# Cosformer attention and MLP-mixer on one core: loading q of batch 4 ahead of its k and v, and q of batch 5 half a period later

## The chip, the cores and the metric

The kernel runs on one core of a Trainium2 chip. The core has a matrix engine (PE, with a row PEld for its weight loads), a vector engine (DVE), a scalar engine (ACT), a general engine (POOL) and SyncE (SP), which here only issues DMAs. The DMAs that SP issues all go out on one hardware queue (q1 in the profile); the stores that POOL issues go out on another (q0). Time is device time in microseconds (us), the median of several runs of the whole program.

## What is computed

For each of 8 batches there are 8 heads of 576 tokens and 64 dimensions. The attention is linear:

```
phi(x) = [relu(x)*cos(theta_s), relu(x)*sin(theta_s)]        theta_s = pi/2 * s/576
kv  = phi(k)^T v          z = sum_s phi(k)                    per head: 128 x 64, 128
x   = phi(q) kv / (phi(q) z + 1e-6)                           576 x 512 per batch
h   = relu(x^T w_tok1) w_tok2                                 token mixing, 576 -> 256 -> 576
u   = x + h^T
out = u + relu(u w_ch1) w_ch2                                 channel mixing, 512 -> 1536 -> 512
```

## The kernel before

**Tiling.** The 576 tokens of a batch are laid out as five tiles (`j` = 0 to 4, `NJ` = 5): four full tiles of 128 tokens, and a tail of 64 that is paired with the tail of the neighbouring batch. A batch of q, k or v is loaded in float32 by `load` (L132) in two DMAs, one of 512 KB for the even partitions and one of 640 KB for the odd ones. Both go through SP.

**Periods.** After a head that works through the first batches, the kernel is a row of periods `g` = 1 to 8, each a list of steps. Period `g` runs channel mixing of batch `g` on PE (`mlp1` at L312, 12 steps, then the second product: `mlp2` at L330 in period 1, `mlp2_unit` at L374 from period 2, a seven-product Strassen-Winograd form on halves whose operand sums are made on DVE by `s_sums`, L354 to L357). Between these products it weaves in the attention and the token mixing of batch `b` = `g`+1 (`num_step`, `b1_step`, `u_step`, `uturn_step`), and the features and the kv product of batch `f` = `g`+2. Counting the head's period `g` = 0 as the first, `g` = 1 is the second period and `g` = 2 the third. Periods are named by `g` from here on.

**Order.** No scheduler moves anything. `plan_of(g)` puts calls into steps with `put(step, function, ...)`, and the calls of a step are issued after that step's matrix product. An engine runs its instructions in the order in which they were issued, and starts one when the semaphores that it waits for are there. So the step number sets the place in each engine's row, and the row, with the waits, sets the time.

**What the steps around the change do.** For batch `f`:

- `q_load`, `k_load`, `v_load` issue the two DMAs of a tensor on SP.
- `qfeat` makes phi(q): the cosine half on DVE (L140), the sine half on ACT (L138). `qturn_dma` (L162) transposes the result by a DMA that SP issues.
- `f1k` makes one half of phi(k), on DVE or ACT (the same lines).
- `vcast` turns a tile of v into bfloat16 on POOL (L156).
- `kv_step` multiplies them on PE (L183), at steps 20 to 25.

For batch `b`, `u_step` adds the token mixing to x on DVE (L255); `uturn_step` casts u on ACT (L260) and transposes it by a DMA on SP (L265). PE needs that transpose, `uT`, for the first product of the next period. `tail_step` and `tail_turn` (L291, L300) handle the paired tails, where `b` is odd. The evictions of `mlp1` to `h1T` are mostly on ACT (L324), in order with its share of `qfeat` and `f1k`.

**Buffers.** q has two raw buffers (batch parity). From batch 4 on, k and v have one raw buffer each, since the second ones then hold the sums of the second product. So a load of v(5) waits until POOL has cast v(4), and a load of v(6) until it has cast v(5).

Of the kernel before, what the change touches and what calls it, by code (L numbers as in the profile page):

```python
# [18 lines left out]
def kernel(  # L19
# [528 lines left out]
    A, V, G = nc.scalar, nc.vector, nc.gpsimd  # L548
# [370 lines left out]
    def plan_of(g):  # L919
        b, f = g + 1, g + 2  # L920
        NS = 24 if g == 1 else 26
        plan = [[] for _ in range(NS)]

        def put(s, fn, *args):
            plan[s].append(lambda: fn(*args))

        if g == 1:
            put(5, tail_step, 1)
            put(19, tail_turn, 1)
            for j in range(NJ):  # L930
                put(j // 2 + 1, f1k, b, j, 0, V)
                put((j + 1) // 2 + 2, kv_step, b, j)
                put(5 + j, num_step, b, j)
            put(3, u_out, 1, 1)
            for n in range(2):
                put(10 + n, b1_step, b, n)
                put(13 + n, u_step, b, n)
                put(13 + n, uturn_step, b, n)
            for j in range(NJ):
                put(8 + j, f1k, f, j, 1, A)  # L940
                put(10 + j, f1k, f, j, 0, V)
                put(8 + j, vcast, f, j, G)
                put(18 + j, kv_step, f, j)
            for j, at in enumerate((12, 15, 16, 17, 18)):
                put(at, q_step, f, j)
            for i in range(4):
                put(19 + i, t_sum, i)
            put(8, v_load, 4)
            put(20, q_load, 4)
            put(22, k_load, 4)  # L950
            return plan
        if b < B:
            for j in range(NJ):
                put(2 + j, num_step, b, j)
            for n in range(2):
                put(8 + n, b1_step, b, n)
                put(12 + n, u_step, b, n)
                put(15 + n, uturn_step, b, n)
            put(18, tail_step, b)
        for at, cs in ((7, (0, 2)), (9, (2, 4)), (11, (4, 5))):  # L960
            put(at, s_sums, *cs)
        if f < B:
            for j in range(NJ):
                put((7, 8, 10, 12, 13)[j], qfeat, f, j, V, A)
                put((7, 8, 10, 17, 17)[j], qturn_dma, f, j)
                put((12, 13, 14, 15, 17)[j], f1k, f, j, 0, V)
                put(13 + j, f1k, f, j, 1, A)
                put(j, vcast, f, j, G)
                put((20, 21, 22, 24, 25)[j], kv_step, f, j)
        if f + 1 < B:  # L970
            put(0, q_load, f + 1)
            put(6, v_load, f + 1)
            put(18, k_load, f + 1)
        return plan

    for g in range(1, B + 1):
        mps = {}
        plan = plan_of(g)
        order = order_of(g)
        for s in range(len(plan)):  # L980
            if s < NCH:
                ps = mlp1(g, order[s])
            elif g == 1:
                t, part = divmod(s - NCH, 3)
                if part == 0:
                    mps[t] = nextM()
                mlp2(g, t, part, mps[t])
            else:
                mlp2_unit(g, s - NCH)
                mlp2_sums(g, s - NCH)  # L990
            for fn in plan[s]:
                fn()
            flush()
            if s < NCH:
                mlp1_out(order[s], ps, V if s in ((11,) if g == 1 else (10,)) else A)
                if g > 1 and s == NCH - 1:
                    s_sums(NQ - 1, NQ)
            elif g == 1 and part == 2:
                mlp2_out(g, t, mps[t], False)
# [33 lines left out]
```

## Time and profile before

| what | value |
|---|---|
| time, median of 5 runs | 263.04 us (263.0 to 263.6) |
| the profiled execution | 263.6 us, its span 261.8 us |
| PE busy | 251.8 us (96% of the span) |
| DVE, ACT, POOL busy | 187.8, 148.2, 97.9 us |
| granted clock of PE | full in all 40 slices |
| DMA | 57.18 MB, mean 218 GB/s |
| one q, k or v batch by SP | 512 KB and 640 KB, median 7.5 to 10.1 us from issue to landing |

A row of the timeline gives start and duration in us, the engine, the line, the operation, what it writes and reads, and how many were merged; the brackets at its end tell how long the engine stood idle before it, and what ended that. A row "SPq" is the time in which SP issues a DMA, not the transfer. In the chain of waits each line is a start, a duration, and the work or wait that the end hangs on at that time.

The periods begin on PE at 87.01 (`g` = 2), 114.62 (`g` = 3), 141.07 (`g` = 4), 167.57 (`g` = 5) and 193.59 us (`g` = 6).

### The profile page before, as it was taken

The numbers are of one execution on the slowest core, as the hardware profiler recorded it, in microseconds if no ns is written. First come the engines' busy times: TensorE is split into PE (matmuls) and PEld (weight loads), VectorE is DVE, ScalarE is ACT, GpSimd is POOL, SyncE is SP. The second block draws the span as 40 slices with busy tenths as digits, with TensorE's granted clock in tenths as the row PEclk, the third lists the DMA queues.
The fourth block names the chain that finished last, engine by engine and source line by source line (L and its number), as shares of the span: only waits on it lengthen the run. The fifth ranks groups of instructions, "written<-read, shape, count | busy, mean of one in ns | idle before, by whom it ended". The sixth has DMA issues, their size and how long they took to land.

```text
span 261.8 us, 5609 instructions
## 1 busy us (share of the span) xinstructions
PE 251.8 (96%) x2074; PEld 154.3 (59%) x2074; DVE 187.8 (72%) x447; ACT 148.2 (57%) x246; POOL 97.9 (37%) x175
## 2 busy tenths in 40 slices
PE   7799999999999999999999999999999999999994
PEld 2465456555545554875586557755875576486483
DVE  5794767696969688939993999489939773563563
ACT  4564586885576429845792679367935452613610
POOL 5178466161142510392039402830291045045041
PEclk9999999999999999999999999999999999999999
DMA  6999999999987999999999997985381034003004
GB/s 193 367 373 384 388 390 384 322 211 262 374 255 168 247 236 356 270 199 326 353 192 147 330 342 157 203 271 100 65 215 70 3 80 162 18 3 150 13 0 162
DMA packets 79947, 57.18 MB, mean 218 GB/s; under 512 B 48176, under 2 KB 74928, under 8 KB 79920
## 3 DMA queue, kind: packets, MB, share of 16 engines
q1 hardware_dynamic: 76128, 47.26, 67.5%
q0 software_dynamic: 2560, 8.39, 9.1%
q10 hardware_dynamic: 1232, 1.18, 1.4%
q8 instruction: 16, 0.26, 0.4%
q14 instruction: 11, 0.09, 0.1%
HBM read 35.85 MB, written 9.44 MB: 173 GB/s over the span
## 4 chain that ended last, share of the span: by engine, by line
PE 67%; DMA 5%; ACT 2%; issue 1%; SPq 1%; DVE 0%; ACTq 0%
PE psM L312 27%; PE psM L374 21%; PE psA L232 4%; PE psM L330 4%; PE psA L250 4%; DMA q_raw<-in_q_dram 3%; PE psA L183 2%; PE psA L207 2%; DMA uT<-u_bf 2%; PE psA L291 1%; ACT u_bf L260 1%; ACT h1T L324 1%; PE psA L374 1%; ACT kp L138 0%; SPq L132 0%
## 5 line engine op out<-in xcount | busy, mean ns | idle before, releaser
L312 PE MATMUL psM<-uT,w_ch 128*128 128x512 bf16 x368 | 88.0, 379 | 0.4 <-DMA uT<-u_bf 0.4
L324 ACT ACTIVATE h1T<-psM 128x512 bf16<-128x512 f32 x93 | 55.4, 597 | 42.6 <-PE psM L312 40.7
L312 PEld LDWEIGHTS <-w_ch 128*128 128x128 bf16 x416 | 38.1, 97 | 40.7 <-issue 0.7
L392 POOL TENSOR_TENSOR res<-res,u_sb 128x256 f32<-128x256 f32 x36 | 26.7, 768 | 78.1 <-DVE res L397 77.7
L156 POOL CAST vb<-v_raw 128x512 bf16<-128x512 f32 (+1 forms) x43 | 23.9, 598 | 23.2 <-DMA v_raw<-in_v_dram 22.8
L138 ACT ACTIVATE kp<-k_raw,sin_t 128x512 bf16<-128x512 f32 (+1 forms) x45 | 28.1, 667 | 1.1 <-DMA k_raw<-in_k_dram 1.1
L138 ACT ACTIVATE qp<-q_raw,sin_t 128x512 bf16<-128x512 f32 (+1 forms) x40 | 26.3, 682 | 4.3 <-DMA q_raw<-in_q_dram 4.3
L374 PEld LDWEIGHTS <-h1T 128*128 128x128 bf16 x252 | 23.8, 97 | 6.2 <-issue 0.6
L374 PEld LDWEIGHTS <-k_raw 128*128 128x128 bf16 x252 | 24.4, 98 | 5.1 <-issue 1.2
L330 PE MATMUL psM<-w_ch,h1T 128*128 128x512 bf16 x96 | 23.8, 379 | 0.0
L374 PE MATMUL psM<-w_ch,h1T 128*128 128x256 bf16 x168 | 22.3, 273 | 0.6 <-ACT h1T L324 0.6
L140 DVE TENSOR_SCALAR kp<-k_raw,cos_t 128x512 bf16<-128x512 f32 (+1 forms) x45 | 20.5, 483 | 1.7 <-DMA k_raw<-in_k_dram 1.7
L255 DVE TENSOR_TENSOR u_sb<-psA,x_sb 128x1024 f32<-128x1024 f32 x16 | 19.5, 1219 | 1.7 <-PE psA L250 1.5
L207 PEld LDWEIGHTS <-qpT 128*128 128x128 bf16 x320 | 14.9, 98 | 9.7 <-issue 1.6
L374 PE MATMUL psM<-w_ch_t,k_raw 128*128 128x256 bf16 x162 | 20.5, 273 | 0.0
L223 DVE TENSOR_TENSOR x_sb<-psA,rden 128x512 bf16<-128x512 f32 x28 | 19.4, 691 | 1.0
L140 DVE TENSOR_SCALAR qp<-q_raw,cos_t 128x512 bf16<-128x512 f32 (+1 forms) x40 | 16.7, 449 | 3.9 <-DMA q_raw<-in_q_dram 3.9
L354 DVE TENSOR_TENSOR k_raw<-h1T 128x512 bf16<-128x512 bf16 (+1 forms) x28 | 9.9, 354 | 11.8 <-ACT h1T L324 11.1
L250 PE MATMUL psA<-B,w_tok 128*128 128x512 bf16 x64 | 16.4, 379 | 0.0
L440 POOL DMA_DIRECT2D out_dram<-res x16 | 8.9, 558 | 19.4 <-DVE res L335 13.6
L219 DVE TENSOR_SCALAR rden<-psA 128x8 f32<-128x8 f32 x35 | 5.7, 163 | 13.7 <-PE psA L207 13.4
L193 ACT CAST kv_sb<-psA 128x520 bf16<-128x520 f32 x7 | 4.2, 603 | 18.9 <-PE psA L183 18.9
(134 smaller groups left out, 378.5 us busy)
## 6 DMA issues: line engine op xcount, KB each, us to landing
out_dram<-res POOLq DMA_DIRECT2D x32, 256.0 KB, 3.5
k_raw<-in_k_dram SPq DMA_DIRECT2D x7, 640.0 KB, 8.6
v_raw<-in_v_dram SPq DMA_DIRECT2D x7, 640.0 KB, 10.1
q_raw<-in_q_dram SPq DMA_DIRECT2D x7, 640.0 KB, 10.0
k_raw<-in_k_dram SPq DMA_DIRECT2D x7, 512.0 KB, 7.5
v_raw<-in_v_dram SPq DMA_DIRECT2D x7, 512.0 KB, 10.0
q_raw<-in_q_dram SPq DMA_DIRECT2D x7, 512.0 KB, 9.4
u_sb<-in_moe_w_ch_dram SPq DMA_DIRECT2D x2, 1024.0 KB, 10.2
```

Source lines behind the costliest of these rows:

```text
L138: eng.activation(out_ap, in_ap, AF.Relu, bias=0.0, scale=s)
L140: eng.tensor_scalar(out_ap, in_ap, scalar1=s, scalar2=0.0, op0=ALU.mult, op1=ALU.max)
L156: eng.tensor_copy(out_ap, in_ap)
L207: nc.tensor.matmul(dst, w, kv_sb[:, h, 0:E1], start=True, stop=True, skip_group_check=True)
L223: nc.vector.tensor_mul(dst.rearrange("p (g h d) -> p g h d", g=2, h=HH), n[:, :, :, 0:D], rb)
L250: nc.tensor.matmul(ps[:, half, :], w2[:, ki, 2 * c + half, :], B1[b % 2][:, ki, :], start=(ki == 0), stop=(ki == NT - 1))
L255: nc.vector.tensor_add(u_sb[b % 2][:, 2 * c:2 * c + 2, :], ps, x_sb[:, 2 * c:2 * c + 2, :])
L312: nc.tensor.matmul(ps.rearrange("p (t k) -> p t k", k=P), wc1[:, ki, mi * P:(mi + 1) * P], src[:, :, ki, :], start=(ki == 0), stop=(ki == ...
L324: eng.activation(h1T[:, mi, :], ps, AF.Relu)
L330: nc.tensor.matmul(ps, h1T[:, ki, t * P:(t + 1) * P], wc2[:, ki, :], start=(ki == 0), stop=(ki == NCH - 1))
L374: nc.tensor.matmul(m[tt][:, tt, :], a[:, c, tt * P:(tt + 1) * P], w[:, c, :], start=(pr < 4 and c == 0 and (tt == 0 or own)), stop=(c == N ...
L392: G.tensor_add(c[:, t, :], s[:, t, :], u[:, t, :])
```

## The change

In period 1, q of batch 4 is loaded at step 8, where v of batch 4 was; k and v of batch 4 are loaded at step 20. In period 2, q of batch 5 is loaded at step 8 instead of step 0, and v of batch 5 at step 18 (ahead of k of batch 5) instead of step 6; the five casts of v of batch 4 are issued at step 12 instead of steps 0 to 4. Periods 3 to 8 keep their plan. Nothing else changes: the instructions on PE, DVE and ACT and their order are the same, on POOL the five casts come behind the two tail copies (L283), and on SP the loads take other places.

```diff
@@ plan_of, g == 1
                 put(at, q_step, f, j)
             for i in range(4):
                 put(19 + i, t_sum, i)
-            put(8, v_load, 4)
-            put(20, q_load, 4)
-            put(22, k_load, 4)
+            put(8, q_load, 4)
+            put(20, k_load, 4)
+            put(20, v_load, 4)
             return plan
@@ plan_of, g > 1
                 put((12, 13, 14, 15, 17)[j], f1k, f, j, 0, V)
                 put(13 + j, f1k, f, j, 1, A)
-                put(j, vcast, f, j, G)
+                put(j if g > 2 else 12, vcast, f, j, G)
                 put((20, 21, 22, 24, 25)[j], kv_step, f, j)
         if f + 1 < B:
-            put(0, q_load, f + 1)
-            put(6, v_load, f + 1)
+            put(8 if g == 2 else 0, q_load, f + 1)
+            put(18 if g == 2 else 6, v_load, f + 1)
             put(18, k_load, f + 1)
         return plan
```

SP's row before, from the end of period 1: turn of the tails, q(4), k(4), q(5), v(5), turns of q(4) tiles 0, 1, 2, turn of u in two halves, turns of q(4) tiles 3 and 4, turn of the tails, k(5), then in period 3 q(6), v(6), turns of q(5). After: turn of the tails, k(4), v(4), turns of q(4) tiles 0 and 1, q(5), turn of tile 2, turn of u in two halves, turns of tiles 3 and 4, turn of the tails, v(5), k(5), then q(6), v(6), turns of q(5).

## The prediction

> **What bounds the kernel now.** I read the page first. PE is busy for 96% of the span at full clock in every slice, so time can only come out of the few places where PE stands. To find them I cut the span at the starts of the periods and asked for the busy time of each stretch; the columns are length, then PE, PEld, DVE, ACT and POOL busy with counts.
>
> ```profile
> PE 251.8 (96%) x2074; PEld 154.3 (59%) x2074; DVE 187.8 (72%) x447; ACT 148.2 (57%) x246; POOL 97.9 (37%) x175
> ...
> 87.01:114.62 27.61, 27.01 (x236) 17.14 (x234) 22.15 (x53) 16.43 (x27) 9.40 (x15) 1.00 1.11 270
> 114.62:141.07 26.45, 26.02 (x231) 17.19 (x232) 21.03 (x51) 17.09 (x28) 9.94 (x17) 1.00 1.10 253
> 141.07:167.57 26.50, 26.50 (x234) 17.15 (x235) 20.99 (x52) 16.92 (x28) 10.58 (x17) 1.00 1.05 250
> 167.57:193.59 26.02, 26.02 (x237) 17.20 (x234) 20.77 (x51) 16.64 (x27) 9.42 (x16) 1.00 0.67 167
> ```
>
> Periods 2 and 4 hold the same work on PE (both have a tail step), yet 2 takes 27.61 us and 4 takes 26.50: period 2 loses 1.11 us. Periods 3 and 5 are the pair without a tail step: 26.45 against 26.02, so period 3 loses 0.43. The chain of waits says what period 2 lost it to.
>
> ```profile
> 88.99 0.61 ACT h1T L324
> 89.60 0.46 SPq L300
> 90.06 0.05 issue
> 90.11 1.26 SPq L132
> 91.37 0.06 issue
> 91.42 6.85 DMA q_raw<-in_q_dram
> ```
>
> q(4) is issued at 90.11 and 91.42, behind the turn of the tails on SP, and lands at 91.42 + 6.85 = 98.27. The timelines of ACT and PE show who stands meanwhile.
>
> ```profile
> 94.23 0.60 ACT L324 ACTIVATE h1T<-psM 128x512 bf16<-128x512 f32 x1 [0.45 <-PE psM L312]
> 98.38 0.72 ACT L138 ACTIVATE qp<-q_raw,sin_t 128x512 bf16<-128x512 f32 x1 [3.55 <-DMA q_raw<-in_q_dram]
> ...
> 101.22 0.71 PE L374 MATMUL psM<-w_ch,h1T 128*128 128x256 bf16 x5 [0.31 <-ACT h1T L324]
> 102.20 0.28 PE L374 MATMUL psM<-w_ch,h1T 128*128 128x256 bf16 x1 [0.27 <-ACT h1T L324]
> ...
> 141.07 2.75 PE L312 MATMUL psM<-uT,w_ch 128*128 128x512 bf16 x12 [0.43 <-DMA uT<-u_bf]
> ```
>
> The first sine half of q(4) holds ACT for 3.55 us, and the evictions of h1T queue behind it. PE has four banks to run ahead in, so it stands only at the second product. The rest of the loss of period 3 is in the last row: a wait for uT.
>
> **The change, part by part.**
>
> *q(4) at step 8 of period 1.* Removed from the path: the wait for q(4). SP issued v(4) at 66.10 to 69.58 in this place, and its two halves took 9.8 and 10.0 us to land, so q(4), of the same sizes, should be there by 79, and nothing asks for it before 94.8. The raw buffer of q(2) has long been read by then. What period 2 gains is read against period 4, stage by stage on PE's timeline: start of period to first L374, 14.21 against 13.73 (0.48 us); that to the first L250, 1.10 against 0.65 (0.45); from there to the first L183, 7.63 in both; from it to the end, 4.67 against 4.49 (0.18). Sum 1.11 us. The last 0.18 is a wait for the turn of u, which is late because ACT is late: the casts of u end 21.95 us into period 2 and 21.07 into period 4. With ACT on time the turn of u's second half is issued at 87.01 + 21.1 = 108.1. Such a turn landed after 2.7 us in period 4 and after 5.2 in period 3, so it lands at 110.8 to 113.3, before the clean end of the period, 87.01 + 26.50 = 113.51. Gain: **1.11 us**, bounds 0.93 (the 0.18 stays) and 1.11.
>
> *k(4) and v(4) at step 20.* SP reaches them where q(4) and k(4) were, at 90.1 and 92.2, so they land as those did: k(4) by 98.3, and v(4), by k(4)'s rows (92.92 plus 8.6), by 101.5. The first feature of k(4) is wanted at about 103.6 and the first kv product at 108.8. Cover of 5 us for k; v has its five casts in between (2.83 us in a row in the later periods), and they end near 104.5. If the load were 4 us later this cover would be gone and PE would wait at L183. Cost 0.
>
> *q(5) at step 8.* It now stands between the turns of q(4) tiles 1 and 2. Those turns depend on the queue: the turn issued at 100.11 held SP for 4.70 us and took 8.8 to land with q(5) and v(5) ahead of it, and the third was issued only at 107.95. After the change only v(4) is ahead of the first one, which is ready at about 97.4; q(5) goes out near 102 and lands by about 107, and SP is free again well before the turn of u at 106.5 (its two halves each 1.2 to 1.3 us). q(5) is not needed before 122. Cost 0, bounds 0 and 0.5 (tile 2's turn holding up the turn of u as it did at 107.95 to 109.19).
>
> *The casts of v(4) at step 12.* They leave 83.61 to 91.6, where one of them held a DVE sum (1.53 us against 0.95 for its equal at L341), but no PE wait hung on that. They now run at about 101.6 to 104.5, beside DVE's busiest stretch. What a POOL operation costs DVE is seen at 95.97: L355, with both inputs in SBUF, took 0.72 instead of 0.42 beside a copy. A feature (L140) took 0.68 instead of 0.48 beside casts at 73.51; evictions from PSUM kept their 0.69. Some 1.1 us of operand sums and two features fall into these casts, so DVE is late by at most 1.1 + 0.4 = 1.5 us. The sums have 1.15 us in hand (in period 3 S2 is done at 130.24, its product starts at 131.39), the casts of u 1.25 (second L255 ends 133.41, its cast on ACT starts at 134.66). Cost 0, upper end 0.3.
>
> *v(5) at step 18, and v(6) behind it.* SP comes to v(5) at about 113.6 (period 4: the turn of the tails ends 26.5 us into it), 4.6 us before it came to k(5), 118.20. It shares the engines with four stores and the turn of the tails, so it lands at about 121. POOL, free at 115.5, waits for it and casts until about 124: no one needs these casts before the kv product at 134.9. But two things follow. First, the casts meet the operand sums of period 3 (122 to 124): four sums by 0.30 and two features by 0.20 make 1.6 us, against 0.36 us of DVE's own idle time before L326 and the 1.15 in hand. I take **0.1 us**; the ends are 0 and, with DVE shut out for all 2.1 us, 0.6. Second, v(6), at step 6 of period 3, waits for the casts, and behind it on SP stand the turns of q(5) and the turn of u(4) that period 3 already waits for. v(6) was issued at 122.06 to 124.0 and landed at 122.76 + 10.1 = 132.9; now it is issued at 124 to 126. That by itself is hidden: k(5) and q(6) are in the queue ahead of it and land about 3.3 us apart (129.6 and 132.9 before), and all started 4.6 us earlier with one load more (3.3). So v(6) should land at 131 to 132.5. The turns of q(5) wait for room in the queue as before, and the turn of u starts when its cast is done, 19.5 and 21.1 us into the period. The wait for uT stays at about 0.4. Cost **0**, ends -0.43 (the wait goes, since that turn took 5.2 us where others took 2.7 to 2.9) and +2.5 (v(6) casts and turns all late).
>
> *A rule against the change.* The Trainium skill, page SBUF — State Buffer, section "SBUF: two separate sides", says that POOL and DVE share one port pair as an exclusive lock, held for a whole instruction, against DVE operations with two SBUF inputs. Its 1.53 us row agrees: 0.58 more beside one cast of 0.62. By the rule the casts of v(5) would take all of the 2.1 us named above, and the sum would be 0.5 us less gain; the rows at 95.97 and 73.51 show a part only.
>
> The sum: -1.11 + 0.1 = -1.0 us. The profiled execution took 263.6 us, span 261.8 and 1.8 around it; by the sum it becomes 262.6. It lies 0.56 above the median of the runs, 263.04, so the median becomes **262.0 us**.
>
> **The rivals.** A measurement of this kernel can tell about 0.2%, 0.53 us, from no change: faster means under 262.5, slower over 263.6.
>
> *DVE eats the gain.* Both sets of casts shut DVE out (0.3 in period 2, 0.6 in period 3), the 0.18 stays: -1.11 + 0.3 + 0.6 + 0.18 = 0.0 at worst, typically -0.3. For it: DVE is busy for nearly all of 122 to 137. Against: 1.15 to 1.6 us in hand in both places. Time 262.6 to 263.1. To this case belongs that the change moves the wait without removing it, with ACT held by something else in its place; nothing on ACT's row before 94.8 suggests one.
>
> *Slower: SP stands at v(6).* v(5) lands late, its casts end late, and the turn of u(4) is caught behind v(6) and the turns of q(5). Clean, period 3 would start at 113.51 and be through with PE's work at 113.51 + 26.02 = 139.53. To lose the 1.11 and 0.53 more, PE must start period 4 at 141.07 + 0.53 = 141.6, so uT must land at 141.46. From the last load's landing to the issue of the second half of u there are a turn of q(5) and the first half (2.5 us), and its landing takes 2.7 to 5.2: v(6) must land after 133.8 to 136.3, that is v(5) some 2 to 4 us later than I have it. For it: the wait exists already and has no slack, and every further us is paid in full. Against: the 4.6 us of head start. Time 263.6 to 265, say 264.2.
>
> *A larger gain.* The uT wait of period 3 goes too: 262.0 - 0.43 = 261.6. It belongs to the forecast's own range, 261.4 to 262.5.
>
> **How the numbers follow.** The forecast has 0.65, DVE (or another wait) eating the gain 0.17, SP standing at v(6) 0.18. Faster 0.65, the same 0.17, slower 0.18. The range goes from 261.3 (both waits gone) to 263.8, which leaves out about 0.03 below and 0.14 of the slower case above.
>
> **What would show it.** Right: ACT goes from the seventh L324 of period 2 to L138 on q(4) without idle time; no PE row of L374 near 101 waits for h1T; period 2 is 26.4 to 26.7 us long; the casts of v(4) start at 101 to 102; v(6) is issued at 124 to 126 and period 3 is 26.0 to 26.6 long. Wrong: L374's third product pair waits for DVE's S2 in period 2 or 3; PE waits for uT at the start of period 4 for over 1 us, with SP standing at L132 on v(6) before it; or v(4) lands after 105 and PE waits at L183.

## The result: 0.34% slower, and the profile after

The changed kernel takes 263.65 us (median of 31 runs, 262.93 to 264.99); the kernel before, on the same chips, 262.82 us (56 runs, 261.93 to 264.01). The ratio is **1.0034, 95% interval 1.0025 to 1.0043**: slower, where 0.4% faster was forecast. Single runs scatter by some 0.5 us (standard deviation) at a granted clock between 0.99 and 1.00, and runs that were much slower at a lower clock are left out of the ratios here and below. The ratio of many runs settles what one profile can't.

The profiled execution of the changed kernel happens to take 263.1 us, span 261.3. Its periods say what the change did. The columns are the stretch, its length, then PE, PEld, DVE, ACT and POOL busy.

```profile
86.61:113.23 26.62, 26.62 (x235) 17.20 (x234) 22.77 (x51) 16.86 (x27) 9.79 (x15) 1.00 1.15 243
113.23:140.52 27.29, 26.18 (x236) 17.22 (x233) 23.07 (x52) 17.36 (x28) 10.87 (x17) 1.00 1.10 280
140.52:167.03 26.51, 26.51 (x234) 17.18 (x235) 20.94 (x51) 16.66 (x27) 11.10 (x18) 1.00 1.02 252
167.03:192.88 25.85, 25.85 (x236) 17.12 (x233) 20.60 (x51) 16.64 (x27) 9.28 (x15) 1.00 0.67 165
```

Period 2 gained nearly what was forecast: 26.62 us instead of 27.61, where 26.50 was expected. Period 3 gave most of it back: 27.29 instead of 26.45. Periods 1, 4 and 5 are the same to 0.01 us in every execution of the two kernels (29.23, 26.51, 25.85; period 5 ends at the first product of period 6, at 193.43 in the kernel before, a row earlier than the prediction took it). So clean values are 26.51 for period 2 and 25.85 for period 3, and period 3 of the kernel before loses 0.60 us, not 0.43.

The gain is where it was looked for. On ACT, the first sine half of q(4) follows the eviction with no idle time:

```profile
93.83 0.60 ACT L324 ACTIVATE h1T<-psM 128x512 bf16<-128x512 f32 x1 [0.45 <-PE psM L312]
94.32 0.71 ACT L138 ACTIVATE qp<-q_raw,sin_t 128x512 bf16<-128x512 f32 x1
```

For the loss, read the rows of SP across period 3. In the kernel before, v(6) goes out right behind q(6):

```profile
122.06 1.94 SPq L132 DMA_DIRECT2D v_raw<-in_v_dram  x2
125.22 8.85 SPq L162 DMA_TRANSPOSE qpT<-qp  x3
134.16 2.80 SPq L265 DMA_TRANSPOSE uT<-u_bf  x2
```

In the changed kernel, SP's rows, then the casts of v(5) on POOL and of u on ACT, then PE's two stalls:

```profile
114.43 1.32 SPq L132 DMA_DIRECT2D v_raw<-in_v_dram  x2
115.84 1.80 SPq L132 DMA_DIRECT2D k_raw<-in_k_dram  x2
117.70 3.18 SPq L132 DMA_DIRECT2D q_raw<-in_q_dram  x2
125.69 1.35 SPq L132 DMA_DIRECT2D v_raw<-in_v_dram  x2
127.14 7.75 SPq L162 DMA_TRANSPOSE qpT<-qp  x3
134.98 3.29 SPq L265 DMA_TRANSPOSE uT<-u_bf  x2
```

```profile
122.67 3.75 POOL L156 CAST vb<-v_raw 128x512 bf16<-128x512 f32 x5 [6.46 <-DMA v_raw<-in_v_dram]
131.72 1.03 ACT L260 CAST u_bf<-u_sb 128x1024 bf16<-128x1024 f32 x1
133.55 1.05 ACT L260 CAST u_bf<-u_sb 128x1024 bf16<-128x1024 f32 x1 [0.18 <-ACT kp L138]
```

```profile
136.30 0.81 PE L374 MATMUL psM<-v_raw,h1T 128*128 128x256 bf16 x6 [0.41 <-DVE res L401]
140.52 2.75 PE L312 MATMUL psM<-uT,w_ch 128*128 128x512 bf16 x12 [0.71 <-DVE res L426]
```

SP has issued q(6) by 120.88 and then stands until 125.69. POOL had to wait for v(5), which landed at 122.55, and only its casts set the buffer free for v(6). Everything behind v(6) is late: the three turns of q(5) hold SP until 134.89, and the halves of the turn of u go out at 134.98 and 136.45, 21.75 and 23.2 us into the period instead of the 19.5 and 21.1 of the kernel before. ACT is not what holds them: its casts of u end 19.5 and 21.4 us into the period, 2.2 and 1.9 us before their turns are issued. In the first profile of the kernel before, each turn went out 0.03 us behind its cast (0.2 to 1.1 us in the other two). The second half took 3.9 us to land, so it was there at 140.38; PE starts at 140.52. The bracket names DVE's L426, which ended about then, but that operation empties the last of the four banks, and the first product needs the first. In the kernel before the same product started 0.14 us behind uT's landing as well (135.72 + 5.21 in its chain, 141.07).

Each of the two kernels was profiled twice more.

> The kernel before, unchanged, for a second profiled execution. If its loss in period 2 is a fixed trait, period 2 is again 27.5 to 27.7 us and period 3 26.4 to 26.5. If the loss depends on when q(4) happens to land, period 2 lies elsewhere between 26.5 and 27.6, and the gain that the prediction took from one execution is too large.

> The changed kernel, unchanged, for a second profiled execution. If its periods are a fixed trait, period 2 is 26.6 and period 3 27.3 us. If DMA timing decides, they move: period 2 up to 27.1 as in the kernel with v(6) at step 18, period 3 between 26.9 and 28.

> The kernel before once more, a third profiled execution: same expectations as for the second one.

> The changed kernel once more, a third profiled execution: same expectations as for the second one.

| execution | span | period 2 | period 3 | sum |
|---|---|---|---|---|
| before | 261.8 | 27.61 | 26.45 | 54.06 |
| before, second | 261.5 | 27.78 | 26.36 | 54.14 |
| before, third | 262.5 | 27.74 | 26.57 | 54.31 |
| after | 261.3 | 26.62 | 27.29 | 53.91 |
| after, second | 262.5 | 27.04 | 27.69 | 54.73 |
| after, third | 261.2 | 26.63 | 27.26 | 53.89 |

So the loss in period 2 is a fixed trait of the kernel before, and the gain there (0.6 to 1.2 us) and the loss in period 3 (0.7 to 1.3 us) are fixed traits of the change. Period 2 of the changed kernel comes in two lengths, 26.6 and 27.04. The longer one is the usual one: all seven kernels below that differ from the changed one only from step 16 of period 2 on have 27.04 or 27.05. In the profiled executions gain and loss cancel on the mean, 54.17 against 54.18; the rest of the spans' scatter is the head, which ends between 57.3 and 58.2 and is untouched by the change. The timed runs put the net at +0.9 us. The second profile, with the usual period 2, shows 0.6 of it (54.73 against 54.17); the rest isn't seen in any profile.

### The profile page after: what moved, and what is told of

The parts are those of the page before. It is cut to its first block, busy times and chain, and to the rows that moved or that the text cites. A ratio compares the mean times of both kernels' runs of the same rounds, so it can differ in the third digit from the quotient of the medians.

```text
span 261.3 us, 5604 instructions
## 1 busy us (share of the span) xinstructions
PE 251.9 (96%) x2074; PEld 154.6 (59%) x2074; DVE 190.1 (73%) x447; ACT 148.7 (57%) x246; POOL 99.6 (38%) x175
## 4 chain that ended last, share of the span: by engine, by line
PE 65%; issue 4%; DMA 3%; POOL 2%; DVE 1%; SPq 0%; ACT 0%; POOLq 0%; ACTq 0%
PE psM L312 27%; PE psM L374 21%; PE psA L232 4%; PE psM L330 4%; PE psA L250 3%; DMA v_raw<-in_v_dram 3%; PE psA L183 2%; PE psA L207 2%; POOL res L392 1%; POOL vb L156 1%; PE psA L291 1%; PE psA L374 1%; DVE res L412 0%; SPq L132 0%; ACT kv_sb L193 0%
## 5 line engine op out<-in xcount | busy, mean ns | idle before, releaser
L156 POOL CAST vb<-v_raw 128x512 bf16<-128x512 f32 (+1 forms) x43 | 25.2, 627 | 34.1 <-DMA v_raw<-in_v_dram 34.1
L255 DVE TENSOR_TENSOR u_sb<-psA,x_sb 128x1024 f32<-128x1024 f32 x16 | 19.5, 1218 | 1.6 <-PE psA L250 1.4
L140 DVE TENSOR_SCALAR qp<-q_raw,cos_t 128x512 bf16<-128x512 f32 (+1 forms) x40 | 17.3, 465 | 2.6 <-DMA q_raw<-in_q_dram 2.6
L354 DVE TENSOR_TENSOR k_raw<-h1T 128x512 bf16<-128x512 bf16 (+1 forms) x28 | 10.7, 383 | 11.4 <-ACT h1T L324 10.7
```

The source lines that it names most:

```text
L140: eng.tensor_scalar(out_ap, in_ap, scalar1=s, scalar2=0.0, op0=ALU.mult, op1=ALU.max)
L156: eng.tensor_copy(out_ap, in_ap)
L255: nc.vector.tensor_add(u_sb[b % 2][:, 2 * c:2 * c + 2, :], ps, x_sb[:, 2 * c:2 * c + 2, :])
```

## The experiments

Lengths of periods are from the profiled execution of each kernel, ratios from its timed runs against the kernel before on the same chip. Four kernels leave work out; their expectations say what.

| kernel | period 2 | 3 | 4 | 5 | ratio to before (95%) |
|---|---|---|---|---|---|
| before (mean of three) | 27.71 | 26.46 | 26.51 | 25.85 | 1 |
| after (mean of three) | 26.76 | 27.41 | 26.51 | 25.85 | 1.0034 (1.0025 to 1.0043) |
| period-2 part alone | 27.34 | 26.94 | 26.51 | 25.85 | 1.0036 (1.0013 to 1.0058) |
| after, v(6) at 18 | 27.04 | 26.49 | 27.48 | 25.86 | 1.0045 (1.0024 to 1.0066) |
| after, v(5) at 13 | 28.22 | 25.85 | 26.51 | 25.85 | 1.0021 (1.0003 to 1.0040) |
| after, v(5) at 16 | 27.04 | 27.32 | 26.51 | 25.85 | 1.0046 (1.0011 to 1.0081) |
| after, v(5) at 17 | 27.04 | 28.95 | 26.56 | 25.85 | 1.0113 (1.0076 to 1.0150) |
| before, q(4) and v(4) early | 28.08 | 26.42 | 26.51 | 25.85 | 0.9996 (0.9973 to 1.0019) |
| before, q(4) at 18 | 27.70 | 26.33 | 26.51 | 25.85 | 1.0007 (0.9985 to 1.0028) |
| before, q(4) early, v(4) at 18 | 28.77 | 26.21 | 26.51 | 25.85 | 1.0045 (1.0023 to 1.0067) |
| before, no load of q(4) | 26.51 | 25.85 | 26.51 | 25.85 | 0.9969 (0.9951 to 0.9988) |
| after, no load of v(5) | 27.04 | 25.86 | 26.51 | 25.85 | 0.9995 (0.9972 to 1.0017) |
| after, no load of v(6) | 27.05 | 25.85 | 26.51 | 25.85 | 0.9992 (0.9970 to 1.0014) |
| after, no early sums in period 3 | 27.04 | 27.53 | 26.60 | 25.85 | 1.0048 (1.0024 to 1.0071) |
| after, q(5) first, v at 18 | 26.70 | 26.54 | 27.25 | 26.42 | 1.0012 (0.9989 to 1.0034) |
| after, v(6) and v(7) at 18 | 27.04 | 26.41 | 27.11 | 26.07 | 1.0020 (0.9992 to 1.0048) |

The theories: **SP** (SP stands at v(6), and the turn of u behind it is late), and its rival, **DVE** (the casts of v(5) hold DVE, whose operand sums PE then waits for).

### Which part of the change costs

```diff
 (before)
-                put(j, vcast, f, j, G)
+                put(j if g > 2 else 12, vcast, f, j, G)
...
-            put(0, q_load, f + 1)
-            put(6, v_load, f + 1)
+            put(8 if g == 2 else 0, q_load, f + 1)
+            put(18 if g == 2 else 6, v_load, f + 1)
```

> Period 1 keeps its old loads (v(4) early, q(4) and k(4) after the turn of the tails); only period 2 has the new places: q(5) at step 8, casts of v(4) at step 12, v(5) at step 18. Both theories expect period 2 to keep its wait for q(4) (27.3 to 27.7 us long) and period 3 to lose what it loses in the changed kernel (27.0 to 27.5 us instead of 26.45): total 0.6 to 1.0 us slower than before. If the loss of the changed kernel has nothing to do with v(5) coming late, period 3 stays at 26.0 to 26.5 and the total is the same as before.

Period 3 grew to 26.94, a little less than expected, period 2 kept its wait for h1T (27.34), and the kernel is 0.36% slower. The cost comes with the period-2 part. The period-1 part, which takes the wait for q(4) away, adds no gain that the timed runs can tell: 1.0036 without it, 1.0034 with it.

### SP standing, or DVE held

First v(6) was moved out of the way, so that SP does not stand in period 3:

```diff
 (after)
-            put(18 if g == 2 else 6, v_load, f + 1)
+            put(18 if g < 4 else 6, v_load, f + 1)
```

> The changed kernel, with the load of v(6) at step 18 of period 3 as well, so that SP does not stand at v(6) ahead of the turns of q(5) and of u(4); the casts of v(5) still meet the operand sums of period 3. Theory 1 (SP stands at v(6)): the turn of u in period 3 is issued on time, about 19.6 and 21.1 us into the period, and period 3 is 26.0 to 26.5 us. Theory 2 (the casts shut DVE out): period 3 stays at 26.8 to 27.4, with PE waiting for DVE at L374. The total is no test by itself, because period 4 then has late casts of v(6) and SP standing at v(7).

Period 3 fell to 26.49, with PE waiting only for DVE, and the loss moved on: in period 4 SP stood at v(7), and that period grew to 27.48. That speaks for SP, with some 0.6 us left over for DVE (26.49 against 25.85). Two kernels that leave work out then took away one cause each:

```diff
 (after: no operand sums at steps 7 and 9 of period 3)
-        for at, cs in ((7, (0, 2)), (9, (2, 4)), (11, (4, 5))):
+        for at, cs in ((7, (0, 2)), (9, (2, 4)), (11, (4, 5)))[2 if g == 3 else 0:]:
 (after: no load of v(6))
-            put(18 if g == 2 else 6, v_load, f + 1)
+            if g != 3:
+                put(18 if g == 2 else 6, v_load, f + 1)
```

> The changed kernel without the operand sums of steps 7 and 9 in period 3: left out are eight DVE operations (L354 to L357 on the first four chunks), so that the casts of v(5) meet next to nothing on DVE; the products of period 3 then work on the sums of period 2. SP still stands at v(6). If SP alone makes the loss of period 3 (27.3 to 27.7 in the changed kernel), it stays at 27.0 or more, with the wait for uT. If the casts that shut DVE out make it, it falls to 25.9 to 26.5.

> The changed kernel without the load of v(6): left out is that transfer alone, batch 6 then works on v of batch 5. SP does not stand, and 1.15 MB less lie ahead of the turn of u in period 3; the casts of v(5) still meet the operand sums. If SP's standing makes the loss, period 3 is 25.9 to 26.1; if DVE makes it, 26.5 (as with v(6) at step 18) or more, with PE waiting for DVE at L401's row. Total 0.8 to 1.4 us below the changed kernel.

Without the sums, DVE has next to nothing to be held from, and period 3 is as long as ever. PE's waits and SP's row in that kernel:

```profile
PE psM L312 <- DMA uT<-u_bf: 1.5, 1, 1.5
```

```profile
125.87 1.31 SPq L132 DMA_DIRECT2D v_raw<-in_v_dram  x2
127.28 8.42 SPq L162 DMA_TRANSPOSE qpT<-qp  x3
135.79 3.18 SPq L265 DMA_TRANSPOSE uT<-u_bf  x2
```

Without v(6), SP goes from q(6) straight to the turns of q(5), the turn of u is issued as soon as its cast is done (19.55 us into the period), and period 3 is clean although the casts of v(5) are there:

```profile
113.67:139.52 25.85, 25.80 (x235) 17.09 (x233) 21.63 (x51) 16.65 (x27) 10.26 (x16) 1.00 1.05 253
```

```profile
119.25 3.48 SPq L132 DMA_DIRECT2D q_raw<-in_q_dram  x2
124.27 8.62 SPq L162 DMA_TRANSPOSE qpT<-qp  x3
133.22 2.80 SPq L265 DMA_TRANSPOSE uT<-u_bf  x2
```

So the load of v(6) in that place is what period 3 pays for. This kernel takes away both the standing and 1.15 MB ahead of the turn of u. The transfer without the standing is in the kernel before, where period 3 is 26.36 to 26.57, and in the kernel with v(5) at 13 below, where it is 25.85: it costs 0 to 0.7 us, and the changed kernel pays 1.4 to 1.8. The rest, by subtraction, is the standing. DVE's share in period 3 is 0 where the casts start 11.6 us into the period, as here, and some 0.6 where they start 9 to 10 us in and SP does not stand (26.41 to 26.54 in three kernels). In the changed kernel the longer wait for uT covers it: without the sums the period was no shorter.

### Can v(5) come earlier?

```diff
 (after)
-            put(18 if g == 2 else 6, v_load, f + 1)
+            put(13 if g == 2 else 6, v_load, f + 1)      (and 16, and 17, in two further kernels)
```

> The changed kernel, with v(5) loaded at step 13 of period 2 instead of 18, so that it is there well before period 3. Both theories expect the casts of v(5) early in period 3, beside evictions from PSUM, v(6) issued on time and period 3 back at 26.0 to 26.5 us. The price would be in period 2: SP waits at v(5) until the casts of v(4) end (104.4), the turn of u goes out behind 1.15 MB, and period 2 may grow from 26.6 to 27.0 or 27.6. Total 0.3 to 1.0 us below the changed kernel, that is from 0.6 below to 0.5 above before.

> The changed kernel, with v(5) loaded at step 16 of period 2, behind both halves of the turn of u and ahead of the turns of tiles 3 and 4 of q(4): some 5 us earlier than at step 18. If the loss of period 3 comes from v(5) being late, its casts run at about 116 to 119 beside evictions from PSUM, v(6) is issued before 121, and period 3 is 25.8 to 26.5 us with period 2 still at 26.6 to 27.0: P2+P3 52.5 to 53.5 against 54.1 to 54.3 in the kernel before; total 0.7 to 1.6 us below before. Risk: the turns of tiles 3 and 4 land late and PE waits for qpT in period 3.

> The changed kernel, with v(5) at step 17 of period 2, behind the turns of tiles 3 and 4 and ahead of the turn of the tails: some 1.5 us earlier than at step 18. By both theories most of period 3's loss stays or goes with each us of v(5): v(5) lands at about 121, casts to 124, half of the loss left: period 3 26.3 to 27.0, total 0.3 to 1.0 us below the changed kernel.

Three places, three different waits. At step 13 period 3 is clean, 25.85, but v(5) now lies ahead of the turn of u(3), and PE pays at the start of period 3. At 16 the turn of u is safe, and the turns of tiles 3 and 4 of q(4) behind v(5) are late. At 17 they are safe too, and PE pays at the start of period 4.

```profile
115.07 2.75 PE L312 MATMUL psM<-uT,w_ch 128*128 128x512 bf16 x12 [1.02 <-DMA uT<-u_bf]
```

```profile
122.48 0.42 PE L207 MATMUL psA<-kv_sb,qpT 128*128 128x65 bf16 x8 [1.03 <-DMA qpT<-qp]
```

```profile
142.35 1.02 PE L312 MATMUL psM<-uT,w_ch 128*128 128x512 bf16 x4 [2.72 <-DMA uT<-u_bf]
```

Step 17 is the miss of this row: v(5) was issued earlier than in the changed kernel, at 113.69, but its second half took 9.9 us (7.4 to 8.9 in the three profiles of the changed kernel) and landed at 124.3, 10.9 us into the period (9.3 to 11.3). Four stores and the turn of the tails ran through the DMA engines at the same time; no run tells which of them held it. SP came to v(6) at 127.33, and the turn of u's second half at 139.41.

The cost follows neither the step at which v(5) stands nor the time of its casts alone (in the second profile of the changed kernel they began later, 11.4 us into the period, and period 3 took 27.69). It goes with the landing of v(6): the second half of the turn of u was issued 2.7 to 3.6 us behind it (4.1 at step 13, where it waited for its cast alone).

| kernel | second half of v(6) lands, us into period 3 | period 3 |
|---|---|---|
| v(5) at 13 | 17.0 | 25.85 |
| before, three profiles | 18.2, 19.3, 18.6 | 26.45, 26.36, 26.57 |
| period-2 part alone | 19.9 | 26.94 |
| after, three profiles | 20.4, 21.1, 20.4 | 27.29, 27.69, 27.26 |
| no early sums in period 3 | 20.9 | 27.53 |
| v(5) at 17 | 22.6 | 28.95 |

Step 16, whose period 3 also waits for the turns of q(4), is not in the table, nor are the kernels of the next section: there v(6) lands 16.7 to 19.5 us into the period, which takes 25.85 to 26.42.

Leaving the load of v(5) out closes the row:

```diff
 (after)
-            put(18 if g == 2 else 6, v_load, f + 1)
+            if g != 2:
+                put(6, v_load, f + 1)
```

> The changed kernel without the load of v(5): left out is that transfer alone, batch 5 then works on v of batch 4. The casts of v(5) run as soon as POOL is free (about 115.7), v(6) is issued without standing, k(5) and q(6) come 1.15 MB earlier. Both theories of period 3 expect 25.8 to 26.2 us for it, and the total 1.0 to 1.6 us below the changed kernel. If period 3 stays above 26.8, v(5) is not the cause.

Period 3 is 25.86, and the total 0.4% below the changed kernel.

### What the wait for q(4) is worth, and other ways to be rid of it

```diff
 (before: no load of q(4))
-            put(20, q_load, 4)
 (before: q(4) early, v(4) stays early)
+            put(8, q_load, 4)
             put(8, v_load, 4)
-            put(20, q_load, 4)
 (before: q(4) ahead of the turn of the tails)
-            put(20, q_load, 4)
+            put(18, q_load, 4)
 (before: q(4) early, v(4) ahead of the turn of the tails)
-            put(8, v_load, 4)
-            put(20, q_load, 4)
-            put(22, k_load, 4)
+            put(8, q_load, 4)
+            put(18, v_load, 4)
+            put(20, k_load, 4)
```

> The kernel before without the load of q(4): left out is that transfer alone, batch 4's attention then works on what the buffer holds (q of batch 2). Nothing waits for q(4), and SP's queue is 1.15 MB lighter. This is the most that freeing period 2 of its wait can bring. If the profiled wait of 1.1 us is there in the timed runs too, the total is 1.0 to 1.7 us below before; if the wait is smaller when the DMAs are not recorded, it is 0.2 to 0.7 below.

> The kernel before with one step moved: q(4) is loaded at step 8 of period 1, ahead of v(4), and both stay there; all else is as before. If the wait for q(4) is worth what the profile of before showed, period 2 goes from 27.6 to 26.5 or 26.6 and the total falls by 0.9 to 1.1 us, with period 3 at 26.0 to 26.5. If period 2's loss is only a trait of the one profiled execution, the total falls by less than 0.5. Risk: the 1.15 MB more between 66 and 82 us hold up the turns of q(3) and of u(2), and period 1 grows.

> The kernel before with one pair of SP's instructions moved by one place: q(4) at step 18 of period 1, ahead of the turn of the tails instead of behind it. q(4) lands about 1.4 us earlier, so ACT stands 2.1 us instead of 3.5 and PE loses 0.2 to 0.6 us in period 2 instead of 1.1; the turn of the tails is not needed for long. Period 2 26.8 to 27.2, period 3 as before; total 0.3 to 0.9 us below before.

> The kernel before with q(4) at step 8 of period 1 and v(4) in its place at the end of the period, at step 18 ahead of the turn of the tails, then k(4); period 2 entirely as before. q(4) is no longer waited for, v(5) keeps its early place and waits only for the casts of v(4), which end near 99. Expected: period 2 26.6 to 27.1 (the casts of v(4) meet operand sums), period 3 as before, 26.0 to 26.5; total 0.4 to 1.1 us below before.

Without the transfer both periods are clean:

```profile
86.69:113.20 26.51, 26.51 (x235) 17.18 (x234) 21.90 (x53) 16.65 (x27) 9.50 (x15) 1.00 1.04 248
113.20:139.05 25.85, 25.85 (x236) 17.12 (x233) 20.60 (x51) 16.64 (x27) 9.28 (x15) 1.00 1.01 249
```

That is 1.8 us less than the kernel before in the profiles, but 0.31% (0.8 us) in the timed runs. The three that keep the transfer each found another wait. With q(4) and v(4) both early, the turn of q(3) comes late behind them:

```profile
95.36 0.42 PE L207 MATMUL psA<-kv_sb,qpT 128*128 128x65 bf16 x8 [1.40 <-DMA qpT<-qp]
```

With q(4) ahead of the turn of the tails, the halves of q(4) went out at 88.64 and 89.33, 1.5 and 2.1 us earlier, but they took 7.4 and 8.5 us to land instead of 6.2 and 6.9, and ACT still stood 3.26 us instead of 3.55. Two stores and the last turn of q(3) were under way beside them; that these held them is likely, not shown. No gain. With v(4) ahead of the turn of the tails, its casts fell on the first operand sums of period 2. The rows of DVE, then of POOL:

```profile
98.56 0.83 DVE L356 TENSOR_TENSOR k_raw<-h1T 128x512 bf16<-128x512 bf16 x1
99.31 2.63 DVE L357 TENSOR_TENSOR v_raw<-h1T,k_raw 128x512 bf16<-128x512 bf16 x1
```

```profile
99.38 2.27 POOL L156 CAST vb<-v_raw 128x512 bf16<-128x512 f32 x4
```

One sum that takes 0.42 us alone took 2.63: it ended 0.29 us behind the last of the four casts in a row beside it. Period 2 grew to 28.77.

### Mending the change

```diff
 (after: v(6) and v(7) at step 18 too)
-            put(18 if g == 2 else 6, v_load, f + 1)
+            put(18, v_load, f + 1)
 (after: that, and q(5) between k(4) and v(4))
-            put(20, v_load, 4)
+            put(22, q_load, 5)
+            put(22, v_load, 4)
...
-            put(8 if g == 2 else 0, q_load, f + 1)
+            if g > 2:
+                put(0, q_load, f + 1)
```

> The changed kernel with the second repair alone: v(6) and v(7) at step 18 of periods 3 and 4. Period 2 stays at 26.6 to 27.0 (casts of v(4) against operand sums), period 3 25.9 to 26.5 without SP standing, period 4 26.5 to 27.0, period 5 25.9 to 26.4. Total 0.4 to 1.2 us below the changed kernel, that is from 0.3 below to 0.4 above before.

> The changed kernel with two repairs. q(5) goes out between k(4) and v(4), so that the casts of v(4) come at about 104.5 to 107.5, behind the operand sums of period 2; and v(6) and v(7) are loaded at step 18 of periods 3 and 4, as v(5) is in period 2, so that SP never stands at a load of v ahead of a turn of u. Expected: period 2 26.5 to 26.9, period 3 25.9 to 26.5, period 4 26.5 to 27.0, period 5 25.9 to 26.4; the sum of the four 104.9 to 106.5 against 106.5 in the kernel before; total 0 to 1.3 us below before. If SP's standing is not what costs period 3, it stays above 27.

With no standing left, period 3 is 26.41 and 26.54, as the SP theory wants, and with q(5) first period 2 is 26.70. But the late casts now meet the operand sums in periods 3, 4 and 5, and there is no longer wait to hide them: period 4 is 27.11 and 27.25 instead of 26.51, above the 26.5 to 27.0 expected, and period 5 26.07 and 26.42 instead of 25.85. The sum of the four periods is 106.6 and 106.9 us against 106.5 in the kernel before. Neither beats it (1.0020, 0.9992 to 1.0048; 1.0012, 0.9989 to 1.0034); no kernel that does all the work did.

## Why the prediction was wrong

**Right.** The wait for q(4) is gone, and so are ACT's idle time and PE's waits for h1T. The 1.11 us for period 2 was measured as 0.7 to 1.1 on the mean of the kernel before (27.71 against 27.04 to 26.62), and 0.7 is the usual value. v(4) landed in time for its kv product, q(5) did not hold the turn of u, and SP came to v(5) at 114.43 (113.6 forecast).

**The casts of v(4), costed at 0 with an upper end of 0.3.** They cost 0.1 to 0.5 us against the clean 26.51, 0.5 in eight of ten executions. The prediction gave DVE 1.15 us in hand and a stretch of 0.30 for a sum of 0.42. (By the rows it is 1.35: S2 is L355 and was done at 130.04, and 130.24 is the end of L356.) The measured stretch is larger. DVE's and POOL's rows of the changed kernel, where the casts begin:

```profile
101.22 0.28 DVE L357 TENSOR_TENSOR v_raw<-h1T,k_raw 128x256 bf16<-128x256 bf16 x1
101.42 0.70 DVE L354 TENSOR_TENSOR k_raw<-h1T 128x256 bf16<-128x256 bf16 x1
102.15 0.58 DVE L355 TENSOR_TENSOR k_raw<-k_raw,h1T 128x256 bf16<-128x256 bf16 x1
```

```profile
101.36 3.08 POOL L156 CAST vb<-v_raw 128x512 bf16<-128x512 f32 x5 [5.35 <-DMA v_raw<-in_v_dram]
```

A sum of 0.28 to 0.29 takes 0.58 to 0.70. Four sums are held in the execution shown; five in the second one, where the casts begin 14.25 us into the period instead of 14.75, and there PE waits 0.33 us at L401's row and period 2 takes 27.04. So v(4) landing *earlier* costs more here. The row at 95.97 had been misread: the copy beside that sum ran from 95.73 to 96.41, and the sum ended at 96.69, so it waited for all that was left of the copy, not for a part. The Trainium skill's rule on the port pair as an exclusive lock (SBUF — State Buffer, "SBUF: two separate sides") was the better guide than this reading. The page speaks of one instruction at a time; the sum of 2.63 us above stayed out for four casts in a row.

**v(5) at step 18, and v(6) behind it: the step that failed.** The prediction had v(5) land at 121, its casts end at 124, v(6) issued at 124 to 126 and landing at 131 to 132.5, and the turn of u "starts when its cast is done". Measured in the three profiles: v(5) landed at 122.55, 125.36 and 123.15; the casts took 3.5 to 3.8 us, held by DVE in turn, and not 2.83; v(6) was issued from 125.69, 128.46 and 126.34 and landed at 133.6 to 135.2. The turn of u did not start when its cast was done: SP stood at v(6) and then at the turns of q(5), and issued it 2.2 and 1.9 us late in the profile shown. Each link was 1 to 5 us late, and the chain had no slack, because the turn of u already set the end of period 3 before the change. The term "Cost 0, ends -0.43 and +2.5" measured +0.7 to +1.3 us against the kernel before, with v(6) away -0.6: inside its ends, but not 0. The head start of 4.6 us on SP, which was to pay for the load more, was 3.8 (114.43 against 118.20) and worth less on the engines: four stores were under way beside v(5), and its second half took 7.4 to 8.9 us.

**The rivals.** "SP stands at v(6)" was right in its place and its mechanism, and its point of decision (v(6) landing after 133.8 to 136.3) was met in one profile and missed by 0.1 to 0.2 us in the other two, whose period 2 had begun 0.4 to 0.5 us earlier; counted from the start of period 2 it was met in all three. It was given 0.18. "DVE eats the gain" is true of 0.1 to 0.5 us in period 2, and in period 3 only once the standing is mended.

**Open.** The profiles say +0.0 us on the mean and +0.6 with the usual period 2, the timed runs +0.9. The three kernels that leave out a load point the same way: by periods they should be 1.3 to 1.8 us below the kernel before, and their timed runs are 0.1 to 0.8 below. In the three kernels that move loads of the kernel before and keep them all, what the periods say and what the timed runs say agree to 0.3 to 0.4 us. So the kernel before seems to lose less to q(4) and uT in a timed run than in its three profiles, and the gain on offer was smaller than the 1.11 us read from one profile. That is inferred from totals; no run shows the periods of a timed execution, and three profiles of each are few against a scatter of 0.5 to 0.8 us.

## What to carry to other kernels

When a load is moved behind a consumer that frees its buffer, follow the issuing queue to the *next* load of that buffer, and read what stands behind it there: an in-order queue turns a late cast into a late transpose two tensors away. A chain that already ends in a wait on the critical engine has no slack, so each link that the change lengthens is to be priced in full and its errors added, not centred on zero. And one profiled execution prices a DMA wait to perhaps half a microsecond: where the forecast gain is of that size, the range has to say so.

## What the runs showed of the hardware

**A later issue slot isn't a later landing.** v(5) issued at 113.69 (step 17) landed at 124.3; issued at 114.43, 115.73 and 113.90 in the three profiles of the changed kernel, it landed at 122.55, 125.36 and 123.15. The same four stores were under way beside it; the turn of the tails was behind it in the first case and ahead of it in the others.

**A gap in the transposes.** The second half of the turn of u in period 3 took 5.2 us to land in the kernel before and 4.6 even in the kernel without q(4), where those of periods 4 to 6 took 2.7 to 2.8. The DMA view of the kernel before, from 137 to 139 us (share of the engines in 40 slices, then the queues):

```profile
DMA  9999999999900000000000000000000000000000
...
q1 hardware_dynamic: 469, 0.12, 181.4%
q8 instruction: 1, 0.02, 6.3%
```

The digits put the whole time of a packet into the slice in which it begins. So for nearly three quarters of these 2 us no packet begins, though a transpose is under way. The packets that began before took long: 469 packets of q1 took 181.4% of 16 engines' 2 us, 124 ns each, against 18 ns in a window of period 4 (162.5 to 164 us: 992 packets, 72.7% of 1.5 us). One packet of instructions was fetched on another queue (q8) at the same time, and took 2.0 us itself (6.3%). Whether the fetch causes the gap was not tried.
